# Pooled attention feeding a two-layer block on one core: the last quarter of group 0's output product moved behind group 1's first pairs of the hidden product

## The chip, the cores and the metric

The kernel runs on one core of a Trainium2 chip. The metric is the device time of one execution in microseconds (us); before the change the median of three runs is 285.82 us (285.27 to 285.86). Engines are named as the profile names them: PE is TensorE's matmul, PEld its weight load, DVE is VectorE, ACT is ScalarE, POOL is GpSimd, SP is SyncE (which only issues DMAs here).

## The reference

Eight batches of eight heads attend to keys and values that are first averaged over runs of eight rows, 576 to 72. The result, as 4608 tokens of 512 features, goes through two matrix products with `h - tanh(h)` between them.

```python
k_p = k.reshape(B, H, Sp, pool, D).mean(axis=3)      # B, H, S, D = 8, 8, 576, 64; pool = 8
v_p = v.reshape(B, H, Sp, pool, D).mean(axis=3)
scores = scale * np.matmul(q, k_p.transpose(0, 1, 3, 2))
attn = softmax(scores)
x = np.matmul(attn, v_p)          # to [4608, 512]
h = x @ w_in                      # 512 x 2048
g = h - np.tanh(h)
out = g @ w_out                   # 2048 x 512
```

## The kernel before

**Groups.** The 4608 tokens are nine groups of 512. Group g below 8 is the first 512 tokens of batch g; the 64 tokens left of each batch form group 8. Each group needs a hidden product (16 hidden tiles of 128, each four matmuls of 128x512 with `w1b`), tanh on ACT, the subtraction on DVE (into `Gt`), and an output product with `w2b`.

**Groups 1 to 8** make hidden tiles in pairs (`h_pair(g, p, b0, ts)`: tiles p and p+8 in two neighbouring PSUM banks from b0, one tanh and one subtraction of 1024 elements for both) and use a Strassen-like output product: seven products instead of eight, on sums of blocks of g (`sum_p`, `sum_q`, `sum_d`, on DVE) and on sums of blocks of `w2b`, made once (`w_sum` into `w2s[0..3]`, `nc.scalar.mul` into `w2s[4]`, and `b12 - ...` in place in `w2b`). Between the products stand the scores and A·V of the next batch.

**Group 0** is the start: `w2s` isn't there yet, so it uses the plain output product `mlp_o(g, tb, qd, gts)`: for each token tile tb (0 to 3) and each quarter qd of the hidden tiles, four matmuls of 128x512. `W2_ORDER = (0, 8, 4, 12)` says which four rows of `w2b` a quarter takes. Quarters must follow the arrival of `w2b`, which comes over GpSimd's queue in pieces. Between them stand batch 1's attention steps, all on PE with copies by DVE and ACT: the turn of pooled k (`k_transpose`), the turn of q (`q_pe_transpose`, `q_pe_tail`), scores and exponentials (`scores_wide`, `scores_ends`), A·V (`av`) and the turn of x (`x_pe_transpose`). During group 0's hidden tiles 5 to 15 the tail of batch 0 is done too: `q_pe_tail(0)` after tile 7 (its copy `qt` on DVE), `scores_tail(0)` after tile 9, `av(0, 4)` after tile 11.

**Pooling.** k and v are pooled by three adds that halve, `pool_k` and `pool_v`; batch 0 and 1 spread pooled v by masks (`v_main`, `v_left`) into `VB`, later batches by DMA (`v_spread`). Batch 1's k is pooled on POOL with the last step on DVE, its v on DVE, the later ones on POOL.

**Order.** The schedule is manual: each engine runs its instructions in the order in which the code issues them, and a waiting instruction holds all that stand behind it on its engine. PSUM has eight banks, handed out by number: `bank(i, shape)`, or in rotation by `Banks(...)`. A matmul into a bank waits until the last reader of that bank is done. `after(loads, dep)` adds a wait by hand. SP issues nearly all loads and the DMA transposes in one queue; loads of `w1b` and `w2b` (with a cast) are on POOL's queue.

The loop that the change takes apart runs sixteen steps u (quarter u // 4, tile u % 4) with the attention steps hung onto them:

```python
for u in range(16):
    qd, tb = u // 4, u % 4
    ...
    if qd == 2:
        for t2 in (2 * (tb % 2), 2 * (tb % 2) + 1):
            mlp_o(0, t2, qd, gts, o_pools[t2], tb // 2 * 2, tb // 2 * 2 + 2)
    else:
        mlp_o(0, tb, qd, gts, o_pools[tb])
```

Of the kernel before, what the change touches and what calls it, by code (L numbers as in the profile page):

```python
# [16 lines left out]
POOL = 8  # L17
# [3 lines left out]
R = 4  # L21
# [22 lines left out]
def kernel(  # L44
# [192 lines left out]
    def halves(n, b):  # L237
        return ((0, n),) if b < 2 else ((0, n // 2), (n // 2, n))

    def pool_k(b, eng, t0=0, t1=NT, mid=(), last=None, dep2=None):  # L240
        r = k_raw[b % 2].rearrange("p t (j d) -> p t j d", d=D)[:, t0:t1, :, :]
        if b not in kdups:
            kdups[b] = work.tile([128, NT, 2, D], BF16, name="kd", tag="kd", bufs=1)
        kd = kdups[b][:, t0:t1, :, :]
        n = t1 - t0
        for ta, tb in halves(n, b):
            eng.tensor_tensor(  # L247
                out=r[:, ta:tb, 0:4, :], in0=r[:, ta:tb, 0:4, :], in1=r[:, ta:tb, 4:8, :], op=ALU.add
            )
        for i, m in mid[0:2]:  # L250
            load_w2(i, m)
        second = eng.tensor_tensor(
            out=r[:, :, 0:2, :], in0=r[:, :, 0:2, :], in1=r[:, :, 2:4, :], op=ALU.add
        )
        if dep2 is not None:
            after([second], dep2)
        for i, m in mid[2:]:
            load_w2(i, m)
        kd_done = (last or eng).tensor_tensor(
            out=kd,  # L260
            in0=r[:, :, 0:1, :].to_broadcast([128, n, 2, D]),
            in1=r[:, :, 1:2, :].to_broadcast([128, n, 2, D]),
            op=ALU.add,
        )
        return kd_done

    def pool_v(b, eng):
        r = v_raw[b % 2].rearrange("p t (j d) -> p t j d", d=D)
        for ta, tb in halves(NT, b):
            eng.tensor_tensor(  # L270
                out=r[:, ta:tb, 0:4, :], in0=r[:, ta:tb, 0:4, :], in1=r[:, ta:tb, 4:8, :], op=ALU.add
            )
        eng.tensor_tensor(
            out=r[:, :, 0:2, :], in0=r[:, :, 0:2, :], in1=r[:, :, 2:4, :], op=ALU.add
        )
        if b < 2:
            eng.tensor_tensor(
                out=r[:, :, 0, :], in0=r[:, :, 0, :], in1=r[:, :, 1, :], op=ALU.add
            )
            v_main(VB[b % 2], r[:, :, 0:1, :], eng, 0, NM)  # L280
            return v_left(VB[b % 2], r[:, NM, 0:1, :], eng)
        if b < 4:
            eng.memset(VB[b % 2][0:G, 0:H, D:D1], float(POOL))
        vps[b] = work.tile([128, NT, D], BF16, name="vp", tag="vp", bufs=1)
        return eng.tensor_tensor(
            out=vps[b][:, :, :], in0=r[:, :, 0, :], in1=r[:, :, 1, :], op=ALU.add
        )

    vps = {}

    def v_spread(b):
        vp, vb = vps.pop(b), VB[b % 2]
        nc.sync.dma_start(out=vb[0:G, 0:H:2, 0:D], in_=vp[0:G, 0:NM, :])
        nc.sync.dma_start(out=vb[0 : 128 - G, 1:H:2, 0:D], in_=vp[G:128, 0:NM, :])
        nc.sync.dma_start(out=vb[128 - G : G, 1:H:2, 0:D], in_=vp[0 : NM * LO, NM, :])

    def v_main(vb, vs, eng, t0, t1):
        n = t1 - t0
        eng.tensor_tensor(
            out=vb[:, 2 * t0 : 2 * t1, 0:D].rearrange("p (t s) d -> p t s d", s=2),  # L300
            in0=vs[:, t0:t1, :, :].to_broadcast([128, n, 2, D]),
            in1=mask[:, 2 * t0 : 2 * t1, :]
# [280 lines left out]

    o_tiles = {}

    def mlp_o(g, tb, qd, gts, pool=None, k0=0, k1=4):
        if qd == 0:
            p, tag = pool or (ps_o, "o_ps")
            o_tiles[tb] = p.tile([128, DM], FP32, name="o_ps", tag=tag)
        o_ps = o_tiles[tb]  # L590
        i0 = W2_ORDER[qd]
        for i in range(i0 + k0, i0 + k1):
            nc.tensor.matmul(  # L593
                o_ps[:, :],
                lhsT=gts[i][:, tb * 128 : (tb + 1) * 128],
                rhs=w2b[:, i, :],
                start=(i == 0),
                stop=(i == NHID - 1),
            )
        if qd == 3:  # L600
            nc.scalar.copy(out=O[:, tb, :], in_=o_ps[:, :])
            if tb % 2:
                store(g, tb - 1, tb + 1, nc.sync)

# [336 lines left out]
    ps_h.n = ps_o.n = 0  # L941
    nc.scalar.copy(out=q_bf[:QT, R, :, :], in_=t0[:QT, :, R, :])
    load_q(1, False)
    load_main(v_pairs, v_raw[1], 1, 0, NM)
    load_q_tail(1, q_raws[1], nc.scalar)
    for i in range(5):
        mlp_h_mms(0, i, 2, 4)
# [1 line left out]


    for i in range(5, NHID):
        mlp_h(0, i, gts, bank((0, 1, 2, 3, 4, 0, 1, 2, 3, 4, 2)[i - 5], [128, TG]))
        if i == 7:
            q_pe_tail(0)
        if i == 9:
            scores_tail(0)
        if i == 11:
            ps_a.n = 0
            av(0, 4, ps_any, True)
            x_dma_transpose(0, 2)  # L960
    kd1 = pool_k(1, nc.gpsimd, mid=((4, 2), (6, 2), (12, 4)), last=nc.vector)
    after([w_sum(w2s[:, 3, :, :], b21, b11, ALU.subtract, nc.gpsimd, k, k + 2) for k in (0, 2)], kd1)
    after(load_k(2), w2_dmas[3])
    load_v(2)

    def q1_cast(t, h):
        nc.scalar.copy(
            out=q_bf[:, 0:R, h : h + 4, :].rearrange("p j h d -> p h j d"),
            in_=t[:, h : h + 4, 0:R, :],
        )  # L970

    o_pools = [(ps_o, "o_ps"), (ps_o, "o_ps"), (ps_h, "hT_ps"), (ps_h, "hT_ps")]
    pend = []
    for u in range(16):
        qd, tb = u // 4, u % 4
        if u == 8:
            scores_wide(1, (3,))
            scores_ends(1)
        if qd == 2:
            for t2 in (2 * (tb % 2), 2 * (tb % 2) + 1):  # L980
                mlp_o(0, t2, qd, gts, o_pools[t2], tb // 2 * 2, tb // 2 * 2 + 2)
        else:
            mlp_o(0, tb, qd, gts, o_pools[tb])
        if u == 0:
            q1 = q_raws.pop(1)
            q1_cast(q1, 0)
        if u == 3:
            k_transpose(1, ps_any, (nc.vector.tensor_copy, nc.vector.tensor_copy))
        if u == 4:
            q_pe_transpose(1, (0, 1), "act")  # L990
            q1_cast(q1, 4)
            nc.scalar.copy(out=q_bf[:QT, R, :, :], in_=q1[:QT, :, R, :])
            load_q(2)
            w_sum(w2s[:, 1, :, :], b11, b12, ALU.add, k1=4)
            w_sum(w2s[:, 0, :, :], b11, b22, ALU.add, k1=4)
            w_sum(w2s[:, 2, :, :], b21, b22, ALU.add, k1=4)
            w_sum(b12, b22, b12, ALU.subtract, k1=4)
            v1_done = pool_v(1, nc.vector)
            after(
                [  # L1000
                    w_sum(w2s[:, 3, :, :], b21, b11, ALU.subtract, nc.gpsimd, k, k + 2)
                    for k in (4, 6)
                ],
                v1_done,
            )
            w_sum(w2s[:, 1, :, :], b11, b12, ALU.add, k0=4)
        if u in (5, 6):
            q_pe_transpose(1, (u - 3,), "act")
        if 5 <= u <= 7:
            scores_wide(1, (u - 5,))  # L1010
        if u == 6:
            q_pe_tail(1)
        if u in (9, 11):
            n = (u - 9) // 2
            nc.scalar.mul(
                out=w2s[:, 4, 4 * n : 4 * n + 4, :], in_=b22[:, 4 * n : 4 * n + 4, :], mul=-1.0
            )
        if 11 <= u <= 14:
            x_pe_transpose(1, *pend.pop(0))
        if 9 <= u <= 12:  # L1020
            pend.append((u - 9, av(1, u - 9, ps_any, False)))
        if u == 13:
            w_sum(w2s[:, 0, :, :], b11, b22, ALU.add, k0=4)
            sums = w_sum(w2s[:, 2, :, :], b21, b22, ALU.add, k0=4)
        if u == 15:
            ps_a.n = 0
            av(1, 4, ps_any, True)
    pool_k(2, nc.gpsimd, dep2=sums)
    pool_v(2, nc.gpsimd)
    w_sum(b12, b22, b12, ALU.subtract, k0=4)  # L1030

    for g in range(1, NG):
        nb = g + 1 if g + 1 < B else None
        nn = g + 2 if g + 2 < B else None
        for p in range(NP - 1):
            c = p if g > 1 else p - 2
            if nb is not None and 0 <= c < 3:
                q_cast_part(nb, c)
            h_pair(g, p, ((2, 0, 4, 6, 0, 2, 4) if g == 1 else (0, 2, 4, 6, 0, 2, 4))[p], p % 2)
            if 3 <= p < 6:  # L1040
                sum_p(2 * p - 6, 2 * p - 4)
            if nb is not None and p == 0:
                k_dma_transpose(nb)
            if g == 1 and p == 0:
                x_dma_transpose(1, 2)
            if g > 1 and p == 0:
                store(g - 1, 2, 4, nc.gpsimd)
                store(g - 1, 0, 2, nc.gpsimd)
            if nb is not None and p == 0:
                k_place(nb, nc.gpsimd.tensor_copy)  # L1050
            if nb is not None and 0 <= c < 3:
                q_dma_transpose(nb, c)
            if nb is not None and c == 2:
                v_spread(nb)
                if nn is not None:
                    load_k(nn)
# [7 lines left out]
        if nb is not None:  # L1064
            sum_d(0, 2)
            sum_d(2, 4)
        ps_a = Banks(2, 3, 4, 5, 0, 1)
        for u in range(14):
            n, half = u // 2, u % 2
            bk, lhs, rhs = products[n]  # L1070
# [57 lines left out]
```

The softmax here doesn't subtract the row's maximum and nothing guards it: scores larger than these inputs give would overflow.

## Time and profile before

| what | value |
|---|---|
| time, median of 3 | 285.82 us |
| span of the profiled execution | 287.5 us |
| PE busy | 276.5 us (96%), 2156 matmuls |
| DVE busy | 221.3 us (77%) |
| ACT busy | 158.0 us (55%) |
| POOL busy | 113.8 us (40%) |
| TensorE clock granted | 1.000 |
| moved by DMA | 50.41 MB, mean 175 GB/s |

The stages of the span, as they stand in the profile's timeline: 0 to 35 us start, batch 0's attention and group 0's hidden tiles; 35 to 56 us group 0's output product with batch 1's attention; 56 to 87 us group 1; from there one full group each 28.8 us up to group 7, then group 8 and the end. A busy PE is not a PE at its peak, since the ends of matmuls are modelled, but an idle one is idle: the four hundredths that are missing in the table are the start, the end, and the stretch from 28 to 74 us. Idle time of the other engines matters only where PE waits for them.

The change keeps all that follows group 1 as it is, apart from line numbers and the rotation of banks in group 1's products.

### The profile page before, as it was taken

How to read it: one execution, taken by the hardware profiler on the slowest of the kernel's cores; microseconds unless marked ns; L12 is line 12 of the kernel's file. 1: busy time of each engine (PE TensorE's matmuls, PEld its weight loads, DVE VectorE, ACT ScalarE, POOL GpSimd, SP SyncE). 2: the span in 40 equal slices, each digit the busy share in tenths (PEclk: the TensorE clock that was granted, in tenths of full speed). 3: DMA queues.
4: the chain of work that ended last, by engine and by line, in shares of the span. 5: the costliest groups of instructions: out<-in, count | busy, mean ns of one | idle time of the engine just before them, and what ended most of it. 6: DMA issues, size and time to landing. Idle time of an engine off the chain costs nothing.

```text
span 287.5 us, 5465 instructions
## 1 busy us (share of the span) xinstructions
PE 276.5 (96%) x2156; PEld 179.7 (63%) x2156; DVE 221.3 (77%) x338; ACT 158.0 (55%) x212; POOL 113.8 (40%) x124
## 2 busy tenths in 40 slices
PE   7799989997999999999999999999999999999994
PEld 3364444643796479647964796479647964884583
DVE  6567878748985898589858985898589838945993
ACT  4637656757817681768176817681768146315510
POOL 8500650794089208920892089208930110000000
PEclk9999999999999999999999999999999999999999
DMA  7999999995997898689859965798560350002014
GB/s 242 229 213 264 308 123 187 328 275 107 295 233 113 222 339 202 85 215 350 191 102 222 355 160 100 227 335 177 101 186 0 51 179 0 2 40 109 0 36 112
DMA packets 67253, 50.41 MB, mean 175 GB/s; under 512 B 42652, under 2 KB 56476, under 8 KB 67228
## 3 DMA queue, kind: packets, MB, share of 16 engines
q1 hardware_dynamic: 57724, 36.04, 50.0%
q0 software_dynamic: 6784, 12.06, 19.9%
q10 hardware_dynamic: 2720, 1.97, 2.4%
q8 instruction: 17, 0.28, 0.4%
q14 instruction: 8, 0.07, 0.1%
HBM read 36.70 MB, written 9.44 MB: 160 GB/s over the span
## 4 chain that ended last, share of the span: by engine, by line
PE 84%; DMA 7%; DVE 3%; ACT 2%; issue 1%; SPq 1%; ACTq 0%
PE PS L665 34%; PE PS L608 34%; PE PS L564 5%; DMA q_raw<-in_q_dram 4%; PE PS L448 3%; PE PS L593 3%; DMA k_raw<-in_k_dram 3%; PE PS L422 3%; DVE Gt L622 2%; PE PS L374 1%; DVE P L630 1%; ACT TS L621 1%; PE PS L463 1%; ACT qT L132 0%; PE PS L844 0%
## 5 line engine op out<-in xcount | busy, mean ns | idle before, releaser
L608 PE MATMUL PS<-xT,w1b 128*128 128x512 bf16 (+1 forms) x504 | 98.1, 355 | 1.5 <-DVE Gt L622 1.5
L622 DVE TENSOR_TENSOR Gt<-PS,TS 128x1024 bf16<-128x1024 f32 x56 | 68.4, 1221 | 35.3 <-ACT TS L621 35.3
L608 PEld LDWEIGHTS <-w1b 128*128 128x128 f16 x576 | 56.3, 98 | 54.3 <-issue 1.8
L621 ACT ACTIVATE TS<-PS 128x1024 f32<-128x1024 f32 x56 | 57.3, 1024 | 29.3 <-PE PS L608 27.1
L709 POOL TENSOR_TENSOR m<-O,m 128x512 f32<-128x512 f32 x6 | 7.6, 1260 | 78.5 <-ACT m L707 78.5
L665 PE MATMUL PS<-w2s,Dg 128*128 128x256 f16 x256 | 30.2, 273 | 0.0
L247 POOL TENSOR_TENSOR k_raw<-k_raw 128x512 f32<-128x512 f32 (+2 forms) x13 | 21.4, 1665 | 18.7 <-DMA k_raw<-in_k_dram 18.7
L443 ACT ACTIVATE E<-PS 72x1024 bf16<-72x1024 f32 (+1 forms) x30 | 26.1, 930 | 4.2 <-PE PS L422 4.0
L665 PEld LDWEIGHTS <-Gt 128*128 128x128 bf16 x256 | 23.5, 98 | 6.8 <-issue 2.3
L665 PEld LDWEIGHTS <-P 128*128 128x128 bf16 x256 | 24.5, 98 | 3.0
L665 PEld LDWEIGHTS <-Dg 128*128 128x128 bf16 x256 | 24.6, 98 | 2.8
L630 DVE TENSOR_TENSOR P<-Gt 128x1024 bf16<-128x1024 bf16 x32 | 22.1, 689 | 0.6
L716 ACT COPY m<-PS 128x512 f32<-128x512 f32 x8 | 4.7, 586 | 29.5 <-PE PS L665 29.5
L640 DVE TENSOR_TENSOR Dg<-Gt 128x1024 bf16<-128x1024 bf16 x32 | 20.4, 683 | 0.0
L681 POOL DMA_DIRECT2D out_dram<-O x14 | 7.7, 552 | 31.7 <-DVE O L719 29.5
L270 POOL TENSOR_TENSOR v_raw<-v_raw 128x512 f32<-128x512 f32 (+1 forms) x12 | 18.2, 1535 | 0.0
L499 DVE TENSOR_TENSOR x_sb<-PS,rden 128x512 bf16<-128x512 f32 x24 | 16.6, 692 | 0.8
L665 PE MATMUL PS<-w2s,Gt 128*128 128x256 f16 x128 | 16.4, 273 | 0.0
L665 PE MATMUL PS<-w2b,P 128*128 128x256 f16 x128 | 16.3, 273 | 0.0
L665 PE MATMUL PS<-w2b,Gt 128*128 128x256 f16 x128 | 16.3, 272 | 0.0
L665 PE MATMUL PS<-w2s,Q 128*128 128x256 f16 x128 | 16.3, 272 | 0.0
L1090 ACT COPY O<-PS 128x512 f32<-128x512 f32 x7 | 4.1, 586 | 21.9 <-PE PS L665 21.9
(120 smaller groups left out, 401.8 us busy)
## 6 DMA issues: line engine op xcount, KB each, us to landing
k_raw<-in_k_dram SPq DMA_DIRECT2D x7, 1024.0 KB, 5.8
q_raw<-in_q_dram SPq DMA_DIRECT2D x7, 1024.0 KB, 10.7
v_raw<-in_v_dram SPq DMA_DIRECT2D x7, 1024.0 KB, 7.9
out_dram<-O POOLq DMA_DIRECT2D x14, 512.0 KB, 3.9
w1b<-in_moe_w_in_dram POOLq DMA_DIRECT2D x4, 512.0 KB, 15.6
w2b<-in_moe_w_out_dram POOLq DMA_DIRECT2D x3, 512.0 KB, 25.3
out_dram<-O SPq DMA_DIRECT2D x2, 512.0 KB, 9.1
k_raw<-in_k_dram SPq DMA_DIRECT2D x7, 128.0 KB, 5.9
```

Source lines behind the costliest of these rows:

```text
L247: eng.tensor_tensor(out=r[:, ta:tb, 0:4, :], in0=r[:, ta:tb, 0:4, :], in1=r[:, ta:tb, 4:8, :], op=ALU.add)
L270: eng.tensor_tensor(out=r[:, ta:tb, 0:4, :], in0=r[:, ta:tb, 0:4, :], in1=r[:, ta:tb, 4:8, :], op=ALU.add)
L422: nc.tensor.matmul(dst, lhsT=kv[a * D : (a + 1) * D, m, :], rhs=rhs, start=True, stop=True,)
L443: nc.scalar.activation(out=e, in_=ps, func=ACT.Exp, scale=SCALE)
L499: nc.vector.tensor_tensor(out=x_sb[:, :, :, :], in0=ps[:, :, :, 0:D], in1=rden[:, :, :, :].to_broadcast([128, 2, 4, D]), op=ALU.mult,)
L564: nc.tensor.matmul(h_tiles[i][:, :], lhsT=w1b[:, fb, i * 128 : (i + 1) * 128], rhs=xT[g][:, :, fb, :], start=(fb == 0), stop=(fb == NFB - 1),)
L608: nc.tensor.matmul(dst[:, t0 * 128 : t1 * 128], lhsT=w1b[:, fb, i * 128 : (i + 1) * 128], rhs=x[:, t0:t1, fb, :], start=(fb == 0), stop=(f ...
L621: nc.scalar.activation(out=t2, in_=PS[:, b0 : b0 + 2, :], func=ACT.Tanh)
L622: nc.vector.tensor_sub(out=Gt[:, p, :, :], in0=PS[:, b0 : b0 + 2, :], in1=t2)
L630: nc.vector.tensor_tensor(out=P[:, a:b, :], in0=Gt[:, a:b, 0, :], in1=Gt[:, a:b, 1, :], op=ALU.add)
L640: return nc.vector.tensor_tensor(out=Dg[:, a:b, :, :], in0=Gt[:, a:b, :, 0:HT], in1=Gt[:, a:b, :, HT:TG], op=ALU.subtract,)
L665: nc.tensor.matmul(part(g, bk, tt), lhsT=lhs(k, slice(tt * 128, (tt + 1) * 128)), rhs=rhs[:, k, :], start=(first and k == 0 and (tt == 0 o ...
```

## The change

It rewrites the stretch between group 0's hidden tiles and the fourth pair of group 1. Its aims are to keep TensorE fed while data arrive, to use VectorE's pauses for sums of weights and for pooling, and to take work from where the next group waits for it. In parts:

1. Batch 1's v is loaded in two halves; the leftover is pooled on DVE after hidden tile 6 is issued, the halves later (`pool_v1`).
2. GpSimd pools k 1 without weight loads in between; rows 4 to 7 of `w2b` come in one piece after rows 8 to 11 have landed, and rows 12 to 15 after two of the weight sums.
3. q of batch 1 is cast in one go; heads 0 to 3 are copied after their turn by DVE, and the turns stand further apart.
4. `mlp_o` takes fixed banks 1, 2, 3, 0; attention gets the four banks 4 to 7 in rotation. A·V of batch 1 takes two banks at a time (`True`).
5. The loop of sixteen steps is written out, with three quarters only. The sums of weights are spread over it.
6. The last quarter, batch 2's q casts and their DMA transposes, the stores of group 0 and batch 3's loads go into `rest_of_group_0()`, ahead of group 1's pair 4. Pairs of group 1 use banks 6, 4, 6, 4, 6, 4, 2.
7. The copies of group 0's output from PSUM are on DVE instead of ACT. `v_spread(2)` is issued by GpSimd.

```diff
     for i in range(5, NHID):
-        mlp_h(0, i, gts, bank((0, 1, 2, 3, 4, 0, 1, 2, 3, 4, 2)[i - 5], [128, TG]))
+        mlp_h(0, i, gts, bank(i % 5, [128, TG]))
         if i == 7:
             q_pe_tail(0)
         if i == 9:
             scores_tail(0)
+        if i == 6:
+            pool_v1(NM, NT)
...
+    ps_a = Banks(4, 5, 6, 7)
+    q1 = q_raws.pop(1)
+    kd1 = pool_k(1, nc.gpsimd, last=nc.vector)
+    load_w2(4, 4)
+    after([w2_dmas[2]], w2_dmas[1])
+    after([w_sum(w2s[:, 3, :, :], b21, b11, ALU.subtract, nc.gpsimd, k, k + 2) for k in (0, 2)], kd1)
+    load_w2(12, 4)
+    w_sum(w2s[:, 1, :, :], b11, b12, ALU.add, k1=4)
+    mlp_o(0, 0, 0, gts)
+    q1_cast(0)
+    q1_cast(4)
+    mlp_o(0, 1, 0, gts)
+    mlp_o(0, 2, 0, gts)
+    k_transpose(1, ps_any, (nc.vector.tensor_copy, nc.vector.tensor_copy))
+    mlp_o(0, 3, 0, gts)
+    mlp_o(0, 0, 1, gts)
+    q_pe_transpose(1, (0, 1), "dve")
+    nc.scalar.copy(out=q_bf[:QT, R, :, :], in_=q1[:QT, :, R, :])
+    pool_v1(0, 2)
+    mlp_o(0, 1, 1, gts)
+    scores_wide(1, (0,))
+    q_pe_transpose(1, (2,), "act")
+    pool_v1(2, 4)
+    mlp_o(0, 2, 1, gts)
+    scores_wide(1, (1,))
+    q_pe_transpose(1, (3,), "act")
+    q_pe_tail(1)
+    w_sum(w2s[:, 1, :, :], b11, b12, ALU.add, k0=4)
+    mlp_o(0, 3, 1, gts)
+    scores_wide(1, (2, 3))
+    scores_ends(1)
+    negated(0)
+    w_sum(w2s[:, 0, :, :], b11, b22, ALU.add, k1=4)
+    mlp_o(0, 0, 2, gts)
+    ps_a.n = 0
+    after(load_k(2), w2_dmas[2])
+    load_v(2)
+    load_q(2)
+    av(1, 0, ps_any, True)
+    av(1, 1, ps_any, True)
+    w_sum(w2s[:, 2, :, :], b21, b22, ALU.add, k1=4)
+    w_sum(b12, b22, b12, ALU.subtract, k1=4)
+    mlp_o(0, 1, 2, gts)
+    turn1(0)
+    mlp_o(0, 2, 2, gts)
+    turn1(1)
+    av(1, 2, ps_any, True)
+    av(1, 3, ps_any, True)
+    w_sum(w2s[:, 0, :, :], b11, b22, ALU.add, k0=4)
+    w_sum(w2s[:, 2, :, :], b21, b22, ALU.add, k0=4)
+    mlp_o(0, 3, 2, gts)
+    turn1(2)
+    turn1(3)
+    av(1, 4, ps_any, True)
...
+    def rest_of_group_0():
+        for n in range(3):
+            q_cast_part(2, n)
+            q_dma_transpose(2, n)
+        for tb in range(4):
+            mlp_o(0, tb, 3, gts)
+        w_sum(b12, b22, b12, ALU.subtract, k0=4)
+        load_k(3)
+        load_v(3)
+        load_q(3)
+        v_spread(2, nc.gpsimd)
...
         for p in range(NP - 1):
+            if g == 1 and p == 4:
+                rest_of_group_0()
...
-            h_pair(g, p, ((2, 0, 4, 6, 0, 2, 4) if g == 1 else (0, 2, 4, 6, 0, 2, 4))[p], p % 2)
+            h_pair(g, p, ((6, 4, 6, 4, 6, 4, 2) if g == 1 else (0, 2, 4, 6, 0, 2, 4))[p], p % 2)
+            if g == 1 and p == 1:
+                negated(1)
...
-        ps_a = Banks(2, 3, 4, 5, 0, 1)
+        ps_a = Banks(*((4, 5, 2, 3, 0, 1) if g == 1 else (2, 3, 4, 5, 0, 1)))
```

In the list of what each engine gets, the change leaves the count of matmuls and of sums alone; it moves them.

## The prediction

> **What bounds the kernel now.** I read the chain of waits first, by line and then in order of time, then the busy time by stage, then the timelines of TensorE (PE) and VectorE (DVE) from 23 to 75 us, and last the DMA issues.
>
> The chain (start, duration, what):
>
> ```profile
> PE 84%; DMA 7%; DVE 3%; ACT 2%; issue 1%; SPq 1%; ACTq 0%
> ...
> 50.29 12.59 DMA q_raw<-in_q_dram
> 62.91 0.04 issue
> ...
> 65.86 0.93 ACT TS L621
> 66.82 1.22 DVE Gt L622
> ...
> 72.32 1.14 DVE Gt L622
> 73.46 0.04 issue
> 73.51 0.41 PE PS L422 x2
> ```
>
> TensorE is the bound (84% of the chain), but at 50 to 73 us the chain leaves it: batch 2's q load lands at 62.9, its cast stands in ScalarE's (ACT) queue ahead of pair 2's tanh, and the pairs of group 1 then run at VectorE's pace.
>
> ```profile
> core 0: us, PE busy (x) PEld busy (x) DVE busy (x) ACT busy (x) POOL busy (x), PEclk, DMA share, GB/s
> 35.00:56.15 21.15, 19.88 (x151) 10.55 (x150) 15.89 (x34) 14.33 (x25) 8.81 (x8) 1.00 1.24 215
> 56.15:74.00 17.85, 15.86 (x89) 8.11 (x87) 12.99 (x15) 11.75 (x15) 11.72 (x12) 1.00 0.87 191
> 87.48:116.30 28.82, 28.82 (x242) 19.71 (x241) 23.77 (x34) 17.11 (x21) 15.20 (x16) 1.00 0.81 210
> ```
>
> Group 2, like each later full group, has TensorE at 28.82 of 28.82 us: nothing to win there, and their code only moves. All that can be won lies in the two stages above.
>
> TensorE's timeline, where it waited (in brackets the idle time and its releaser):
>
> ```profile
> 28.87 0.42 PE L374 MATMUL PS<-qt,KB 128*128 128x64 bf16 x8
> 41.94 0.40 PE L216 MATMUL PS<-ident,q_bf 128*128 128x128 bf16 x4 [1.02 <-ACT q_bf L967]
> 45.74 0.44 PE L374 MATMUL PS<-qt,KB 128*32 128x64 bf16 x8
> 69.91 1.89 PE L608 MATMUL PS<-xT,w1b 128*128 128x512 bf16 x8 [1.49 <-DVE Gt L622]
> 73.51 0.41 PE L422 MATMUL PS<-qT,KB 64*72 64x512 bf16 x2 [0.50 <-DVE Gt L622]
> ```
>
> A 128x512 matmul issues every 0.216 us (16 of them from 34.84 to 38.29), so a wait is a start minus the end of issue before it. From 28.8 to 73.84 (second half of product 0) I get 0.08 (28.87), 1.19 (41.94), 0.41 (45.74), 0.57 (three small ones on VB and E, 47.7 to 51), 1.63 (69.91) and 0.6 (73.51): 4.48 us. No change of order can bring more.
>
> ```profile
> 23.62 4.87 DVE L577 TENSOR_TENSOR Gt<-PS,TS 128x512 bf16<-128x512 f32 x8 [1.74 <-ACT TS L575]
> 28.41 0.41 DVE L134 CAST qt<-PS 128x256 bf16<-128x256 f32 x1
> ```
>
> ```profile
> L270 DVE TENSOR_TENSOR v_raw<-v_raw 128x1280 f32<-128x1280 f32 x1 | 1.5, 1492 | 1.6 <-DMA v_raw<-in_v_dram 1.6
> L273 DVE TENSOR_TENSOR v_raw<-v_raw 128x640 f32<-128x640 f32 x1 | 0.8, 826 | 0.0
> L277 DVE TENSOR_TENSOR v_raw<-v_raw 128x320 f32<-128x320 f32 x1 | 0.5, 492 | 0.0
> L309 DVE TENSOR_TENSOR VB<-v_raw,mask 128x256 bf16<-128x256 f32 x1 | 0.4, 420 | 0.0
> ```
>
> The first fence is VectorE's timeline (start, duration, engine, line, operation, what ended its idle time), the second the groups by form (last number before the bar's end: mean ns of one). Eight subtractions run back to back, one per 0.61 us, until 28.49; the qt copy follows at once and TensorE takes qt 0.05 us after its end. VectorE has no pause there.
>
> **What the Trainium skill says.** "VectorE: DVE Perf Modes" (Mode 1×) gives an fp32 tensor_tensor one element per cycle of 0.96 GHz: the rows above have 1.04 ns an element and 0.16 us fixed. "Perfetto Trace Analysis" (Matmuls) asks that independent matmul groups rotate through different PSUM banks so that evacuation overlaps; group 1 will have two pairs of banks only, and I price that below. "SBUF — State Buffer" (two separate sides) says that VectorE instructions with two SBUF inputs and GpSimd (POOL) instructions lock each other out of a shared port pair: the trace agrees, a weight sum takes 0.68 us alone and 1.35 us at 57.27 beside GpSimd's adds.
>
> **The change part by part.** Times are on the profile's clock.
>
> (1) The leftover of v 1 (four VectorE instructions) goes between the subtractions of hidden tiles 6 and 7. They cost 0.43, 0.29 and 0.23 (256, 128, 64 elements by the rows above) and 0.42, with 0.03 between dependent ones less 0.08 of overlap: 1.38 us. Queued behind them are subtraction 7 and the qt copy, and TensorE waits for qt at the tail scores with every later hidden tile behind it. Those scores go from 28.87 to 30.25: 1.38 us lost on the path, and mlp_o starts at 36.22 instead of 34.84.
>
> (2) GpSimd's second add of k 1 no longer waits for two weight issues, q's casts come together, and qT 0 and 1 are copied by VectorE. Twelve quarters of 0.864, k turn 0.28, q turns 0.23 each: q heads 0 to 3 turn at 40.8, after their cast (38.34 + 1.04); the second cast ends at 40.3. The 1.19 and the 0.41 fall away (four rotating banks instead of three). The scores end at 45.81.
>
> (3) Quarter 2 of tile 0 ends at 46.68. A·V block 0 takes bank 4, where the last of four exponentials stands: they start at 45.30 and end 1.91 later (45.09 to 47.00 before): wait 0.58. Blocks 0 and 1, quarter 2 of tiles 1 and 2 and turns 0 and 1 follow. Block 3 takes banks 4 and 5, so it waits for ScalarE's copy of turn 1: 0.50. Turn 3 waits 0.17 for block 3's scaling. Pair 0 takes banks 6 and 7, which turns 2 and 3 just filled: two copies, 0.60. With 0.03 more, pair 0 starts at 53.8.
>
> (4) Pairs use banks 6 and 4 in turn. Pair 2 needs bank 6 after pair 0's tanh and subtraction: 0.26 + 1.02 + 0.03 + 1.23 + 0.05 = 2.59 us, of which pair 1 hides 1.73: wait 0.86. Pair 3 then just meets its bank.
>
> (5) The last quarter (16 x 0.216 = 3.46) stands between pairs 3 and 4, at 61.6 to 65.1, and is the same work as before. Batch 2's casts (0.94 + 0.94 + 0.6 of ScalarE) are hidden by it; q lands by about 60, since its load starts some 2.5 us sooner. So the 1.63 and the 0.6 go, if VectorE keeps up: pair 3's subtraction 62.9, one P sum, four output copies (0.61 each, a PSUM source like L499), the w2b sum 67.1, pair 4's subtraction 68.1, pair 6's 71.6 to 72.8. Head scores need that at 73.2: 0.3 us to spare. The copies leave ScalarE, where nobody waited.
>
> (6) Weight sums: the same eight. Those that meet GpSimd's sums or pooling are stretched, up to 0.67 each by the row at 57.27; before block 2's scaling and pair 1 I take 0.15 of it on the path, 0 to 0.7 as bounds.
>
> (7) w2 rows 4 to 7 are issued after rows 8 to 11 landed, at 37.7 instead of 34.1, in one piece. Needed at 45.8 by TensorE, and at 46.1 by a weight sum with A·V's scaling behind it. In the trace of before the two pieces issued at 34.1 and 34.8 landed at 45.4 and 47.1 (11.3 and 12.3 us), but all DMA together moved only 18 GB/s from 40 to 43; rows 4 to 7 flowed in the last 3.6 us alone. Issued at 37.7 behind v, I estimate 44 to 46: no wait. Bounds: 42 and 48.
>
> (8) Stores of group 0 go after q's transposes, near 66; the output buffer is written again at 76. Such stores took 9.1 us beside loads and 3.9 without: 0, at most 1 us.
>
> Sum: waits of after 1.38 + 0.08 + 0.58 + 0.03 + 0.50 + 0.17 + 0.60 + 0.86 = 4.20, and 0.15 of lock-out: 4.35, against 4.48. Gain 0.13 us: 285.82 becomes 285.7.
>
> **The rivals.** *Faster:* part (1) is hidden, as the idea of pauses has it, or the four instructions take their short end. Then 1.38 comes off: 285.7 - 1.4 = 284.3. For it: q's stall and the pairs' stall are real and do go. Against: VectorE's eight subtractions without a gap and qt taken at once. *Slower by weights:* rows 4 to 7 land at 47 to 48 as the second piece did. TensorE waits 1.2 to 2.2, of which 0.58 overlaps the exponentials, and the scaling starts 1 us later: 286.7 to 287.3. For it: 12.3 us to landing before, and a later issue now. Against: v competes less once the older rows have landed. *Slower by VectorE:* copies at 0.69 and the w2b sum at 1.35 add 1 us to a queue with 0.3 to spare, and the lock-out takes its upper bound: 286.6. For it: pairs 4 to 6 have their subtractions queued behind five other instructions. Against: in the copies' time the quarter feeds no subtraction.
>
> **How the numbers follow.** Balance 0.40 (285.7), hidden leftover 0.30 (284.3), late weights 0.18 (287.0), VectorE 0.12 (286.6). 0.2% is 0.57 us. The first case, spread by some 0.4 us of unpriced hops, stays within in nine of ten cases; a few late-weight cases too. Faster 0.32, same 0.39, slower 0.29. The range 284.2 to 287.3 takes in the three other cases and leaves a tenth on each side.
>
> **What would show it.** Right: tail scores near 30.2 with a wait for the VectorE copy of qt; no wait on q's cast after 40; waits at A·V block 0 on the exponentials, at pair 0 on the turns' copies, at pair 2 on pair 0's subtraction; no wait from pair 4 to the products; second half of product 0 near 73.7. Wrong: tail scores still at 28.9 (faster), a wait on w2b at 45.8, or a VectorE wait after pair 6 (slower), or any idle time of TensorE in groups 2 to 7.

## The result, and the profile after

The changed kernel takes 290.37 us (median of 4 runs, 289.02 to 290.85) against 285.84 us of the kernel before on the same chip: ratio 1.0148, 95% interval 1.0102 to 1.0193. It is slower by 1.5%, outside the predicted range. A later set of runs gave 289.75 us (289.17 to 290.50) and 1.0140 (1.0106 to 1.0175). In two of the sets below one execution of five ran in a slower state, with a lower mean clock (0.996 and 0.988), and is left out of the median.

TensorE's timeline of the changed kernel, where it waited, first execution (start, duration, engine, line, operation, in brackets the idle time before it and its releaser; lines have moved, L613 is `h_mms`, L469 A·V, L380 scores):

```profile
25.52 1.89 PE L570 MATMUL PS<-xT,w1b 128*128 128x512 bf16 x8
28.71 0.42 PE L380 MATMUL PS<-qt,KB 128*128 128x64 bf16 x8 [1.30 <-DVE qt L134]
...
45.59 0.86 PE L469 MATMUL PS<-VB,E 128*128 128x130 bf16 x12 [0.33 <-ACT E L413]
...
49.36 0.34 PE L469 MATMUL PS<-VB,E 128*128 128x130 bf16 x3 [0.15 <-ACT xT L555]
...
51.50 1.96 PE L613 MATMUL PS<-xT,w1b 128*128 128x256 bf16 x16
55.46 7.03 PE L613 MATMUL PS<-xT,w1b 128*128 128x512 bf16 x24 [2.00 <-DVE x_end L505]
62.32 3.62 PE L598 MATMUL PS<-w2b,Gt 128*128 128x512 f16 x16
65.77 7.07 PE L613 MATMUL PS<-xT,w1b 128*128 128x512 bf16 x32
...
88.56 6.75 PE L613 MATMUL PS<-xT,w1b 128*128 128x256 bf16 x38 [0.72 <-DMA xT<-x_sb]
```

The tail scores wait 1.30 us for the qt copy, as predicted. From 62.32 (the last quarter) to group 1's last pairs there is no wait, as predicted. But at 55.46 stands a wait for which step (6) had only 0.15 us: pair 1 waits 2.00 us for VectorE's scaling of A·V block 4, whose banks 4 and 5 it takes.

The timeline of the same execution at that place, GpSimd's adds of batch 2's k beside VectorE's sums of weights:

```profile
50.26 1.81 POOL L247 TENSOR_TENSOR k_raw<-k_raw 128x768 f32<-128x768 f32 x1
50.78 3.79 DVE L653 TENSOR_TENSOR w2s<-w2b 128x1024 f16<-128x1024 f16 x2
...
52.15 1.86 POOL L250 TENSOR_TENSOR k_raw<-k_raw 128x640 f32<-128x640 f32 x1
...
54.09 1.87 POOL L253 TENSOR_TENSOR kd<-k_raw 128x640 bf16<-128x640 f32 x1
```

and VectorE's own timeline, with what stands behind the two sums:

```profile
54.71 0.69 DVE L505 TENSOR_TENSOR x_end<-PS,rden 128x512 bf16<-128x512 f32 x1
55.32 1.21 DVE L627 TENSOR_TENSOR Gt<-PS,TS 128x1024 bf16<-128x1024 f32 x1
```

Two sums that take 0.68 us each alone (1.28 us for two in a row) need 3.79 us, 1.84 for the first and 2.02 for the second. The first is issued while GpSimd's add of 50.26 runs (to 52.07), the second at about 52.5, soon after the add of 52.15 began (to 54.01): each ends some 0.5 us after the add that it met. That two such instructions hold each other up is called the lock below. The scaling of block 4 stands behind the two sums and ends at 55.4, where TensorE goes on. The kernel before had a wait by hand against part of this, `pool_k(2, nc.gpsimd, dep2=sums)`: GpSimd's second add waited for the two sums. The change drops it.

The same execution by stretches of 1 us (busy shares, then the granted clock in the third column from the right):

```profile
core 0: us, PE busy (x) PEld busy (x) DVE busy (x) ACT busy (x) POOL busy (x), PEclk, DMA share, GB/s
...
55.00:56.00 1.00, 0.54 (x3) 0.29 (x3) 1.00 (x2) 0.00 (x0) 1.00 (x2) 1.00 0.55 116
56.00:57.00 1.00, 1.00 (x5) 0.34 (x3) 0.54 (x1) 0.00 (x0) 1.00 (x1) 0.72 0.29 58
57.00:58.00 1.00, 1.00 (x4) 0.40 (x3) 0.00 (x0) 0.00 (x0) 1.00 (x2) 0.50 0.09 15
58.00:59.00 1.00, 1.00 (x4) 0.33 (x3) 0.00 (x0) 0.82 (x1) 0.94 (x1) 0.50 0.32 61
59.00:60.00 1.00, 1.00 (x4) 0.35 (x3) 0.76 (x1) 1.00 (x2) 0.00 (x0) 0.57 0.53 103
60.00:61.00 1.00, 1.00 (x6) 0.43 (x5) 0.46 (x1) 0.35 (x2) 0.79 (x3) 1.00 0.00 0
```

After the pause the clock is down to a half for some 3 us: a stretch of 1 us touches 4 matmuls there, and 6 at full clock (one that spans an edge counts in both). From pair 1 to the last quarter, 55.46 to 62.32, the 24 matmuls take 6.86 us; in the second profile (below), at full clock and with a wait of 0.69 us for pair 2's bank, they take 6.03. So the half clock costs 0.8 us beyond the wait that it hides. It is not what makes the kernel slower: the three other executions had a mean clock of 0.998 or 0.999 and still took 289.0 to 290.8 us.

One thing must be known of the profile that the prediction read: that execution of the kernel before took 289.25 us itself, 3.4 us more than the median of its timed runs. Two later profiles of it have spans of 284.7 and 284.8 us. Part of the difference lies at the start, ahead of all that the change touches: TensorE waited there for batch 0's pooled k, which it did not do in the two later ones, and group 0's output product began at 34.84 us instead of 33.43 and 33.42.

```profile
10.99 0.29 PE L328 MATMUL PS<-ident,kd 128*128 128x128 bf16 x2 [1.81 <-DVE kd L259]
```

TensorE's waits after the start in the second of the three:

```profile
40.52 0.40 PE L216 MATMUL PS<-ident,q_bf 128*128 128x128 bf16 x4 [1.02 <-DVE w2s L648]
...
54.20 14.00 PE L608 MATMUL PS<-xT,w1b 128*128 128x256 bf16 x72
...
84.38 10.90 PE L608 MATMUL PS<-xT,w1b 128*128 128x256 bf16 x57 [0.85 <-DMA xT<-x_sb]
```

and in the third:

```profile
40.51 0.40 PE L216 MATMUL PS<-ident,q_bf 128*128 128x128 bf16 x4 [1.02 <-ACT q_bf L967]
...
67.07 1.89 PE L608 MATMUL PS<-xT,w1b 128*128 128x512 bf16 x8 [0.60 <-DVE Gt L622]
...
70.66 0.41 PE L422 MATMUL PS<-qT,KB 64*72 64x512 bf16 x2 [0.50 <-DVE Gt L622]
```

The wait at q's turn is in all three (1.02). The wait of 1.49 us in group 1 is 0 and 0.60 here, the 0.50 at the head scores is 0 and 0.50. They went with the time at which batch 2's q landed (62.9 us in the first execution, 60.0 in the third, 59.0 in the second). Of the 3.01 us of these waits in the first execution, 0.9 to 2.0 us belonged to that execution.

### The profile page after: what moved, and what is told of

Its sections match the earlier page's. It is cut to its first block, busy times and chain, and to the rows that moved or that the text cites. A ratio compares the mean times of both kernels' runs of the same rounds, so it can differ in the third digit from the quotient of the medians.

```text
span 289.1 us, 5457 instructions
## 1 busy us (share of the span) xinstructions
PE 278.0 (96%) x2155; PEld 180.1 (62%) x2156; DVE 225.7 (78%) x343; ACT 155.1 (54%) x206; POOL 116.4 (40%) x126
## 4 chain that ended last, share of the span: by engine, by line
PE 85%; DVE 6%; DMA 4%; ACT 2%; issue 1%; SPq 0%; ACTq 0%; DVEq 0%
PE PS L613 38%; PE PS L670 33%; PE PS L598 4%; PE PS L428 3%; PE PS L454 3%; PE PS L570 2%; DMA xT<-x_sb 2%; DMA k_raw<-in_k_dram 2%; DVE Gt L583 2%; DVE w2s L653 1%; DVE x_sb L505 1%; PE PS L380 1%; PE PS L469 1%; PE PS L849 0%; PE PS L216 0%
## 5 line engine op out<-in xcount | busy, mean ns | idle before, releaser
L613 PE MATMUL PS<-xT,w1b 128*128 128x512 bf16 (+1 forms) x504 | 100.1, 359 | 2.7 <-DVE x_end L505 2.0
L613 PEld LDWEIGHTS <-w1b 128*128 128x128 f16 x576 | 56.6, 99 | 57.1 <-issue 4.5
L505 DVE TENSOR_TENSOR x_sb<-PS,rden 128x512 bf16<-128x512 f32 x28 | 19.4, 691 | 1.0
L722 DVE TENSOR_TENSOR m<-m,m 128x512 f32<-128x512 f32 x8 | 11.9, 1493 | 5.2 <-ACT m L721 5.2
```

The source lines that it names most:

```text
L505: nc.vector.tensor_tensor(out=x_sb[:, :, :, :], in0=ps[:, :, :, 0:D], in1=rden[:, :, :, :].to_broadcast([128, 2, 4, D]), op=ALU.mult,)
L613: nc.tensor.matmul(dst[:, t0 * 128 : t1 * 128], lhsT=w1b[:, fb, i * 128 : (i + 1) * 128], rhs=x[:, t0:t1, fb, :], start=(fb == 0), stop=(f ...
L722: nc.vector.tensor_tensor(out=m4, in0=m4, in1=m45, op=ALU.subtract)
```

## The experiments

Each was built on the changed kernel unless it says otherwise. Times are medians, and the ratio is to the kernel before on the same chip. The second profile of the kernel before, above, came with a control: the kernel before once more.

> The kernel before, timed against itself: ratio 1.000 within its interval, and a second profile of it. All theories expect that. It says how far one profile of an unchanged kernel lies from another: the first loads landed 1.55 us apart in the two profiles at hand, so a start that differs by 1 to 2 us belongs to the run and not to the change.

It took 285.79 us, ratio 1.0000 (0.9985 to 1.0015). VectorE's timeline in it:

```profile
51.95 4.00 DVE L648 TENSOR_TENSOR w2s<-w2b 128x1024 f16<-128x1024 f16 x2
...
56.10 0.69 DVE L499 TENSOR_TENSOR x_end<-PS,rden 128x512 bf16<-128x512 f32 x1
```

The kernel before has the stretched sums too (4.00 us here, 3.40 in the third profile), in spite of its wait, which guards only against GpSimd's second add. There they cost nothing: its pair 1 takes banks 0 and 1, and in this execution its TensorE runs 72 matmuls from 54.20 without a gap. In the first profile they took 1.28 us, so the prediction saw only one stretched sum (1.35).

### Holding GpSimd back

```diff
-    w_sum(w2s[:, 2, :, :], b21, b22, ALU.add, k0=4)
+    sums = w_sum(w2s[:, 2, :, :], b21, b22, ALU.add, k0=4)
...
-    pool_k(2, nc.gpsimd)
+    pool_k(2, nc.gpsimd, dep1=sums)      # both halves of the first add wait
```

> The kernel after, with GpSimd's first adds of batch 2's k made to wait for the two VectorE weight sums that stood at 50.8 us. Lock-out theory (GpSimd's adds hold up the sums, these hold up the scaling of A.V block 4, whose banks pair 1 needs, and the wait cools TensorE's clock): the two sums take 1.3 us instead of 3.8, pair 1 starts without a wait, the clock stays at 1.00 from 55 to 61 us, pair 2 waits some 0.9 us for its bank, and the time falls by 2.5 to 3.5 us from the changed kernel's. Rival (the loss is the early wait of 1.3 us at the tail scores and later transfers, the pair 1 wait is made up for afterwards): within 1 us of the changed kernel.

287.76 us, 1.0071 (1.0055 to 1.0088): 2.6 us of the 4.5 are back, or 2.0 against the later set of runs. VectorE's timeline:

```profile
51.22 1.28 DVE L657 TENSOR_TENSOR w2s<-w2b 128x1024 f16<-128x1024 f16 x2
...
52.65 0.69 DVE L509 TENSOR_TENSOR x_end<-PS,rden 128x512 bf16<-128x512 f32 x1
```

The same two sums take 1.28 us, x_end is scaled 2.1 us earlier on the trace's clock, and pair 1 doesn't wait. Now pair 2 does, for its bank, as step (4) had it (0.70 measured, 0.86 predicted):

```profile
56.33 3.61 PE L617 MATMUL PS<-xT,w1b 128*128 128x512 bf16 x16 [0.70 <-DVE Gt L631]
```

### Pool the leftover of v 1 later

```diff
-        if i == 6:
-            pool_v1(NM, NT)
...
         if i == 9:
             scores_tail(0)
+            pool_v1(NM, NT)
```

> The kernel after, with the pooling of the leftover of v 1 on VectorE moved from behind hidden tile 6 to behind the tail scores (tile 9). Pause theory: the copy of qt comes 1.3 us earlier, the wait of 1.3 us at the tail scores goes, and 1.3 us come off, unless a later wait takes them back. Rival (a later wait on data, the weights or q, takes it back): the tail scores start on time and the time does not move by more than 0.4 us.

> Both edits, the guard on GpSimd's adds and the leftover of v 1 behind tile 9. If the two losses are independent, their gains add: 3.8 to 4.8 us less than the changed kernel, which is 0 to 1.5 us less than the kernel before. If one wait only gives way to the next, the sum is clearly less than the two apart.

Alone: 290.66 us, 1.0190 (1.0142 to 1.0238), no gain. With the guard: 287.12 us, 1.0059 (1.0039 to 1.0080), 0.64 better than the guard alone where 1.3 were at stake. The timeline of the first of the two says why:

```profile
29.77 2.89 POOL L247 TENSOR_TENSOR k_raw<-k_raw 128x1280 f32<-128x1280 f32 x1 [16.08 <-DMA k_raw<-in_k_dram]
...
29.86 3.08 DVE L315 TENSOR_TENSOR VB<-v_raw,mask 128x256 bf16<-128x256 f32 x1
...
32.86 0.68 DVE L583 TENSOR_TENSOR Gt<-PS,TS 128x512 bf16<-128x512 f32 x1
```

The leftover's last instruction was issued 0.09 us after GpSimd's first add of k 1 and ended 0.28 us after it: 3.08 us instead of 0.43. Tail scores no longer wait, but the subtractions behind it do, and TensorE with them:

```profile
33.59 1.02 PE L570 MATMUL PS<-xT,w1b 128*128 128x512 bf16 x4 [0.94 <-DVE Gt L583]
...
38.15 0.45 PE L334 MATMUL PS<-ident,kd 128*128 128x128 bf16 x5 [0.64 <-DVE kd L253]
```

0.94 and 0.64 in place of 1.30. It isn't enough to move an instruction out of one queue's way; the new place must be free of the other engine too. So the leftover went to where GpSimd waits for weights (40 to 45 us), in exchange for two sums:

```diff
     pool_v1(2, 4)
+    pool_v1(NM, NT)
...
-    w_sum(w2s[:, 1, :, :], b11, b12, ALU.add, k0=4)
...
-    w_sum(w2s[:, 0, :, :], b11, b22, ALU.add, k1=4)
...
             h_pair(g, p, ...)
+            if g == 1 and p == 1:
+                w_sum(w2s[:, 1, :, :], b11, b12, ALU.add, k0=4)
+            if g == 1 and p == 2:
+                w_sum(w2s[:, 0, :, :], b11, b22, ALU.add, k1=4)
```

> The changed kernel with the leftover of v 1 pooled after the second half of v 1 instead of after hidden tile 6; the two weight sums that stood there go behind the subtractions of group 1's pairs 1 and 2. Theory A (the earlier try to move the leftover gained nothing only because its last step met GpSimd's first add of k and took 3.1 us instead of 0.43): at about 44 us GpSimd waits for weights, the leftover takes 1.4 us, and PE's 1.30 us at the tail scores are won: 288.6 to 289.2 us. Rival B (VectorE has no slack anywhere from 26 to 46 us, so the leftover costs its 1.4 us wherever it stands): 289.8 us or more.

289.7 us, 1.0134 (1.0088 to 1.0180): between the two theories. The 1.30 is gone, and waits of 0.45 (for x of batch 1) and 0.16 (for VB) came up; pair 1 still waits 1.99 and pair 2 0.69. At half the expected size this run settles nothing by itself.

### Take away who waits, not the lock

The last quarter goes ahead of pair 1 instead of pair 4, and the banks of the pairs and of group 1's products change with it; the sums stay where GpSimd stretches them.

```diff
+            if g == 1 and p == 1:
+                for tb in range(4):
+                    mlp_o(0, tb, 3, gts)
             if g == 1 and p == 4:
                 rest_of_group_0()              # without its mlp_o
...
-            h_pair(g, p, ((6, 4, 6, 4, 6, 4, 2) if g == 1 else ...
+            h_pair(g, p, ((6, 4, 2, 6, 0, 2, 4) if g == 1 else ...
```

> The changed kernel with the four tiles of group 0's last quarter ahead of group 1's pair 1 instead of pair 4, and the pairs on banks 6, 4, 2, 6, 0, 2, 4. The two weight sums are left where GpSimd's adds lock them out, so they should still take about 3.8 us. Theory A (the sums cost time only because pair 1 needs the two banks of A.V block 4, whose scaling stands behind the sums): the quarter's 3.45 us of matmuls now lie between the sums and pair 1, so the 2.0 us wait goes, and so does the 0.7 us wait of pair 2 for a bank; first product 3.4 to 3.9 us earlier than in the changed kernel, time 286.4 to 287.0 us. Rival B (the locked-out sums hold VectorE, and VectorE's backlog reaches PE wherever the quarter stands): the wait moves to pair 2 or 3 and the time stays above 288.5 us.

287.9 us, 1.0073 (1.0054 to 1.0092): 2.5 us back, 1 us less than expected. VectorE's sums are as long as ever:

```profile
51.09 3.94 DVE L653 TENSOR_TENSOR w2s<-w2b 128x1024 f16<-128x1024 f16 x2
```

but the waits of pairs 1 and 2 are gone, and two new ones stand at the end of the group:

```profile
68.09 1.89 PE L613 MATMUL PS<-xT,w1b 128*128 128x512 bf16 x8 [0.51 <-DVE Gt L627]
...
71.69 0.41 PE L428 MATMUL PS<-qT,KB 64*72 64x512 bf16 x2 [0.50 <-DVE Gt L627]
```

Two edits come to 287.8 and 287.9: one takes the lock away, one leaves it and moves the quarter's 3.45 us of matmuls between the sums and the one that waits for them. So the stretched sums cost this time because pair 1 comes too soon behind them, on banks that stand behind them in VectorE's queue. The kernel before, with pair 1 on banks 0 and 1, agrees; other banks for pair 1 with all else left in place were not tried.

Both edits together, and the guard on top:

> Both of these edits together. If the two waits are separate costs, both gains add: 285.0 to 285.6 us, so no slower than the kernel before (285.8). If VectorE's backlog is the limit, the two sums that were moved behind pairs 1 and 2 come back as waits of pairs 3 to 6, and the time is 286.5 us or more.

> The same with GpSimd's first adds of k of batch 2 also held back until the two weight sums are done. If with the quarter ahead of pair 1 nobody waits for the sums any more, the guard is worth nothing: within 0.3 us of the kernel without it. If the sums still cost something, up to 1 us faster. It could also be slower, by GpSimd's later pooling, if batch 2's k or v then comes late.

287.55 us, 1.0052 (1.0034 to 1.0070), and with the guard 288.33 us, 1.0088 (1.0057 to 1.0119). The gains don't add, and the guard does harm here. GpSimd's pooling starts later with it and meets more of the sums moved behind pairs 1 and 2, which took 0.68 and 1.42 us without the guard. VectorE's timeline with it:

```profile
61.08 1.04 DVE L657 TENSOR_TENSOR w2s<-w2b 128x1024 f16<-128x1024 f16 x1
...
63.18 2.02 DVE L657 TENSOR_TENSOR w2s<-w2b 128x1024 f16<-128x1024 f16 x1
```

The late pair then waits 1.29 us instead of 0.51. The lock was moved, not removed.

### The two new waits: VectorE's copies or ScalarE's casts

First the copies of group 0's output back on ACT (`nc.scalar.copy` in `mlp_o`), on the quarter alone and on both edits:

> The quarter ahead of pair 1, and the copies of group 0's output on ACT again (as in the kernel before) instead of VectorE. In the run without this edit VectorE was 2.5 us longer busy with the copies, and PE waited 0.51 us for the subtraction of a late pair and 0.50 us at the head scores. Theory A (the copies on VectorE, together with the 3.8 us of locked-out sums, are that backlog, while ACT stands idle for 4 us there): both waits go, 0.7 to 1.0 us faster than the quarter alone (287.9): 286.9 to 287.2 us. Rival B (VectorE's backlog comes from the sums alone): within 0.3 us of 287.9.

> The same with the leftover of v 1 pooled after the second half of v 1, and the two sums behind pairs 1 and 2. Theory A: the 0.9 us at the end of group 1 go here too: 286.5 to 286.8 us. Rival B: no gain, 287.5 us.

288.17 us, 1.0092 (1.0076 to 1.0107), and 287.97 us, 1.0081 (1.0064 to 1.0098): nothing gained, so theory A fell in both. In the first, 0.51 and 0.49 stayed although VectorE was 2.5 us less busy. The chain of waits of the first of the two, in order of time:

```profile
63.42 1.41 ACT q_bf L184 x2
...
65.31 0.62 ACT q_bf L189
65.92 0.93 ACT TS L626
...
66.87 1.22 DVE Gt L627
```

It goes through ScalarE: batch 2's three q casts stand in one piece ahead of pair 4's tanh. In the changed kernel the last quarter lies beside them (step 5); with the quarter gone to pair 1 nothing does. So the casts and their transposes were spread, one before each of pairs 1 to 3, and the second half of `w2s[4]` was negated after pair 0 instead of pair 1:

```diff
-        for n in range(3):
-            q_cast_part(2, n)
-            q_dma_transpose(2, n)
...
-            if nb is not None and g > 1 and p < 3:
-                q_cast_part(nb, p)
+            c = p if g > 1 else p - 1
+            if nb is not None and 0 <= c < 3:
+                q_cast_part(nb, c)
```

> The quarter ahead of pair 1 with the copies on ACT and the q casts spread over pairs 1 to 3; leftover of v 1 and sums of weights stay as in the changed kernel. Theory A: 1.0 us faster than with the casts in one piece (288.17): 287.0 to 287.3 us, and what is left against the kernel before is the leftover's 1.3 us at the tail scores. Rival B: 287.9 us or more.

286.84 us, 1.0033 (1.0011 to 1.0056): 1.33 faster than with the casts in one piece. No late pair waits, and at the head scores 0.18 us are left. The leftover's 1.30 at the tail scores stands, and there are waits of 0.48 and 0.44 for x of batch 1. (The profiled execution took 288.72 us, with 1.63 us of waiting for batch 0's k at the start, as in the first profile of the kernel before.) The edit holds two moves, the casts and the negation; the trace above points to the casts, but they were not tried alone.

### All sums behind A·V block 4

On the version with the leftover moved, the quarter first and the copies on ACT, the sums between the A·V scalings went behind the last of them (the lines that go are left out here):

```diff
     av(1, 4, ps_any, True)
+    w_sum(w2s[:, 1, :, :], b11, b12, ALU.add, k0=4)
+    w_sum(w2s[:, 0, :, :], b11, b22, ALU.add)
...
             if g == 1 and p == 1:
                 for tb in range(4):
                     mlp_o(0, tb, 3, gts)
+                w_sum(w2s[:, 2, :, :], b21, b22, ALU.add)
+                w_sum(b12, b22, b12, ALU.subtract)
```

> The same, and all sums of weights on VectorE that stood between the A.V scalings of batch 1 go behind the scaling of A.V block 4: two before pair 0's subtraction, two (each over all eight rows) behind the last quarter. Theory A (the waits of 0.49 and 0.44 us for x of batch 1 come from a locked-out sum of 1.64 us that stands ahead of those scalings): they go, 285.5 to 286.2 us, the kernel before reached. Rival B (the sums meet GpSimd's adds in their new place as well, 1 to 2 us each, and hold up the subtractions of group 1): 287 us or more.

> The version with the leftover after v's second half, the quarter ahead of pair 1, copies on ACT and the sums behind A.V block 4, with batch 2's q casts and their transposes spread over pairs 1 to 3 instead of in one piece at pair 4. Theory A (the casts in one piece hold pair 4's tanh for 2.6 us, and that comes out as the two waits of 0.5 us): both go, 285.5 to 285.9 us, equal to the kernel before. Rival B (the waits come from VectorE's sums): no change, 286.7 us.

286.70 us, 1.0043 (1.0026 to 1.0059): the two waits for x are gone, as theory A had it, the two late ones stayed (0.50 and 0.49), and the time lies between the two theories. With the casts spread these go too: 286.05 us over 22 runs, 0.9993 (0.9979 to 1.0007), no different from the kernel before. All that the change lost is found again, and nothing is won. In that kernel the first two sums take 4.46 us:

```profile
51.35 0.69 DVE L505 TENSOR_TENSOR x_end<-PS,rden 128x512 bf16<-128x512 f32 x1
51.95 4.46 DVE L653 TENSOR_TENSOR w2s<-w2b 128x1024 f16<-128x1024 f16 x2
```

The second of the two is over all eight rows (2.56 us of the 4.46), so this is not to be set beside the pairs of sums above. They are stretched here too, but x_end is scaled ahead of them. What VectorE's queue still costs is 0.52 us at one pair, where three subtractions stand behind the two sums moved to the last quarter.

### Once more: what belongs to the kernels, what to one execution

> The kernel before, unchanged, a third profile. Theory A (the waits of 1.49 and 0.50 us for the last pairs of group 1 were those of one execution, in which batch 2's q landed at 62.9 us): they are missing, and the span is 284 to 285.5 us. Rival B (they belong to the kernel and the second profile was the odd one): PE waits about 1.5 us before group 1's pair 6 or 7 again.

286.62 us for this single execution, span 284.8. Neither theory holds as it stands: of 1.49 and 0.50 a part is there (0.60 and 0.50, shown above). These waits vary from one execution to the next.

> The changed kernel, unchanged, a second profile and more times. Theory A (the half clock at pairs 1 and 2 was that of one execution): granted clock 1.00 at the pairs, waits of 1.3 us at the tail scores, 2.0 at pair 1 and then 0.7 at pair 2, and the time is again 289.0 to 290.9 us. Rival B (the pause of 2 us at pair 1 makes the clock fall each time): half clock for some 3 us after the pause.

289.75 us, 1.0140. TensorE's timeline of the second profile:

```profile
29.12 0.42 PE L380 MATMUL PS<-qt,KB 128*128 128x64 bf16 x8 [1.30 <-DVE qt L134]
...
54.99 3.61 PE L613 MATMUL PS<-xT,w1b 128*128 128x512 bf16 x16 [1.12 <-DVE x_end L505]
59.29 1.89 PE L613 MATMUL PS<-xT,w1b 128*128 128x512 bf16 x8 [0.69 <-DVE Gt L627]
```

Here the sums took 2.90 us and pair 1 waited 1.12; the clock stayed at 1.00, and pair 2 waited its 0.69. The leftover's wait is the same to the hundredth; the lock's varies with where GpSimd's adds fall.

## Why the prediction was wrong, step by step

Two terms failed. The first is step (6): "before block 2's scaling and pair 1 I take 0.15 of it on the path, 0 to 0.7 as bounds". TensorE stood idle 2.00 and 1.12 us at pair 1 in the two profiles, and 2.0 to 2.6 us of run time came back when the lock alone was taken away. What was wrong in it is the size. 0.67 per sum came from one row in which a sum met the tail of an add; a sum that meets an add near its start waits for most of it, here 1.16 and 1.34 us on top of 0.68 for two in a row. The Trainium skill, "SBUF — State Buffer", section "Who interferes with whom", says that who issues first holds the pair for the whole instruction, and that issue order decides who blocks; the traces agree (29.77 against 29.86 above). The bound should have been the length of GpSimd's adds (1.3 to 2.9 us in the trace of before), not the one stretch seen. The diff also removes `dep2`, which no step priced. Whether that cost anything is not shown: the two sums took 1.28, 4.00 and 3.40 us with it in the three profiles of the kernel before, 3.79 and 2.90 without it, and it was not put back alone. The lock as such cost nothing in the kernel before; the change put pair 1 on the banks of A·V block 4, whose scaling stands behind the sums. No sign of being wrong in the prediction names pair 1.

The second is the balance, the 4.48 us on its side of before. These waits were those of one execution, and its span (287.5 us) stood above the median time (285.82), which can't be for a typical one. From the start of group 0's output product to the second half of product 0 that execution took 39.00 us (34.84 to 73.84), the two later ones 36.46 (33.43 to 69.89) and 37.58 (33.42 to 71.00). So 1.4 to 2.5 us of the 4.48 were not there to be won.

The other steps. The prediction counted a wait from the end of issue, which gives 0.1 to 0.2 us more than the brackets; its way of counting is used here.

- (1) Right: 1.38 predicted on top of 0.08; measured 1.46 in both profiles (28.71 less 25.52 and 8 x 0.216). The scores came at 28.71 and 29.12, not at 30.25, since the start was earlier than in the execution that the prediction read.
- (2) No wait for q after 40 us: right.
- (3) 1.85 us of waits at A·V and pair 0 predicted, 1.11 measured (0.49, 0.32 and 0.30). Pair 0 did not wait for the turns' copies, for which 0.60 stood in the sum. Too dark by 0.7 us, which hid part of step (6).
- (4) Right: 0.86 predicted, 0.84 measured where the clock was full (59.29 less 54.99 and 16 x 0.216).
- (5) Right: no wait from the last quarter to group 1's end. The experiments add that the casts in one piece are hidden only with the quarter beside them.
- (7) Right: no wait for `w2b`; where TensorE came 1.3 us earlier, with the quarter first and the leftover later, it waited 0.19.
- (8) Within its bound, if the 0.72 and 0.42 us at group 2's start are put to it. The second profile of before has 0.85 at the same place, so this is not counted as a loss.

For the changed kernel itself the forecast was near: 36.22 to 73.7, 37.5 us, for the stretch named above, and 37.89 measured in the second profile, with 1.35 at pair 1 instead of 0.15 and 0.7 less in step (3); that these two nearly cancel is luck. In the first profile, with 2.23 at pair 1 and the half clock, it took 39.60. "Slower by VectorE" (286.6, chance 0.12) named the right engine with too small a lock. Not all of the loss is seen in the traces: the medians differ by 4.1 to 4.5 us, while the profiled executions of 289.17 and 286.62 us, one below the median of its set and one above, differ by 2.55, and their waits in brackets by 1.9 (4.01 and 2.12). The rest lies in executions without a trace. The experiments account for it only in sum: the quarter first with the copies on ACT and the casts spread brings 3.5 us back (290.37 to 286.84), the leftover and the sums together another 0.8 (to 286.05).

## What to carry to other kernels

When VectorE instructions with two SBUF inputs can meet GpSimd's adds, bound each by the whole length of the other's instruction, and then look who stands behind it and which banks the next matmuls take: in these runs a stretched sum was free as long as no matmul needed what was queued after it. And before waits are counted as a gain, compare the span of the profiled execution with the timed runs.

## What the runs showed of the hardware that was not expected

After a pause of 2.00 us TensorE's granted clock fell to 0.50 for about 3 us in one execution; after 2.00 and 1.99 us in two other kernels (leftover behind the tail scores, leftover behind v's second half) it stayed at 1.00. The Trainium skill, "TensorE: Matmul & The Clock Gate", section "Part 1: The HAM clock gate", gives the half clock for after at least one idle window of about 3.4 us. The one execution differs from that: a pause of 2.00 us was enough. The page also calls the window free-running, so the place of a pause within it might count; no run here tests it.
